# V of an attention kernel through a padded DRAM buffer by head group, in place of four SBUF blocks

## The chip, the cores and the metric

One core of a Trainium2 chip. The metric is device time in microseconds (us) of one execution. The kernel before took 3974.69 us (median of 3 runs, 3971.6 to 3993.35).

## The reference

Two layers, each an attention block and then an MLP block with Mish, on S = 2048 rows of D = 512, in float32 throughout:

```python
x = A_x
x = x + _A_ref(_layernorm(x, axis=-1), A_wqkv, A_wo)
x = x + _B_ref(_layernorm(x, axis=-1), B_w1, B_b1, B_w2)
x = x + _A_ref(_layernorm(x, axis=-1), A_wqkv, A_wo)
x = x + _B_ref(_layernorm(x, axis=-1), B_w1, B_b1, B_w2)
...
# _A_ref: H = 32 heads of Dh = 16
qkv = (lambda x, *d: x.transpose(*d))((x @ wqkv).reshape(B, S, 3, H, Dh), 2, 0, 3, 1, 4)
scores = jnp.einsum("bhqd,bhkd->bhqk", q, k) * (Dh ** -0.5)
p = _softmax(scores, axis=-1)
o = jnp.einsum("bhqk,bhkd->bhqd", p, v)
return (lambda x, *d: x.transpose(*d))(o, 0, 2, 1, 3).reshape(B, S, D) @ wo
```

## The kernel before

**Blocks.** Most of SBUF is one pool, `blk`: 22 blocks of 8 KB a partition (`NBLK`, handed out by `b8`). Normalized x, weights, K and Q of a head group, V, attention output, residuals and exponentials all take their tiles from it. Which block a tile gets, and so which earlier reader it waits for, is settled when the program is built; a scheduler then also sets the order on each engine, except where the code chains PE's instructions one behind the other (`pe`), as it does from the first max matmul of an attention to its end.

**QK stage.** `qkv` computes Q and K transposed, splits each result into a high and a low part, and writes them to DRAM (`scr`, 512 KB a tile, issued by ACT). `prep_qk(g)` loads K and Q of head group g back from there, by SP: two `ks` and two `qs` blocks for a group of four heads (`HG`); there are eight groups (`NG`).

**V stage.** `qkv` ends with V: 16 row tiles of 128 rows (c = 0..3, t = 0..3), each 12 matmuls into a PSUM bank, and one ACT copy. Four tiles share one block `v{l}{c}`. The four blocks live to the last head group, since `prep_v(g)` takes from them the columns of its group: into a fresh block `va` that POOL first zeroes (L232) and gives a column of ones a head (L233, which yields the softmax denominators), it copies four pieces (L235). Each head has 32 columns there (`VW`), 16 of them V.

**Attention.** `run` goes through 512 steps a layer: eight groups of 64, each 4 blocks of 512 queries (qb) by 16 key tiles (kt). A step is four heads' scores for one kt and qb. `CYCLE` writes out the order by hand: P, a pair of score matmuls `sp` and one exponential over both (L312); S, a single score `ss` and its exponential (L322); M, a max matmul `pm` and its maximum on DVE (L265), which run 24 steps ahead (`AHEAD`); v, the product of exponentials and va (`pv`, L339), two steps behind the scores. Each tile `p` holds three heads' exponentials and takes one block; its number is that of its first head, so `p0486` is layer 0, head 486, and the tile before is `p0483`. The maxima of 16 steps are folded on DVE (`nm`, L272), transposed on PE (`nmt`, L282), split on DVE (`np`) and loaded into rows of `qs` by eight small DMAs of SP (L289).

**Group switch.** In steps 32 to 63 of a group `prep_qk` loads the next group's four blocks; at step 48 `prep_v` fills the next va. The old group's ks, qs and va come free when its last steps have been done. During these last 16 steps the pool holds ks and qs of two groups, two va, four output blocks and four v blocks. In the last group the v blocks are done with, and weights of Wo and W1 and the residuals come in instead.

Of the kernel before, what the change touches and what calls it, by code (L numbers as in the profile page):

```python
# [9 lines left out]
F32 = mybir.dt.float32  # L10
F32R = mybir.dt.float32r
BF16 = mybir.dt.bfloat16
AF = mybir.ActivationFunctionType
# [5 lines left out]
P = 128  # L19
S, D, H, DH, F = 2048, 512, 32, 16, 1792  # L20
NCH = 4
CW = S // NCH
KT = D // P
NKT = S // P
FT = F // P
HG = 4
NG = H // HG
VW = 32
# [21 lines left out]
def kernel(ctx: ExitStack, tc: tile.TileContext, x, wqkv, wo, w1, b1, w2, out):  # L50
    nc = tc.nc
# [7 lines left out]
    dram = ctx.enter_context(tc.tile_pool(name="dram", bufs=1, space=DRAM))  # L59
# [13 lines left out]
    def b8(shape, dt, name):  # L73
        return blk.tile(shape, dt, tag="blk", name=name)
# [13 lines left out]
    def pbank(tag, name):  # L88
        if tag == "s":
            return banks["s"].tile([P, 512], F32, tag=tag, name=name, bufs=3)  # L90
        return ps.tile([P, 512], F32, tag=tag, name=name, bufs=1)
# [32 lines left out]
    def split_psum(hi, lo, src):  # L124
        nc.scalar.activation(hi, src, AF.Copy)
        nc.vector.tensor_tensor(lo, src, hi.bitcast(F32), op=ALU.subtract)

    def mm3(acc, pairs, first=True, last=True, pe=lambda ins: ins):
        n = len(pairs)
        for i, (ah, al, bh, bl) in enumerate(pairs):  # L130
            pe(nc.tensor.matmul(acc, ah, bh, start=first and i == 0, stop=False))  # L131
            pe(nc.tensor.matmul(acc, ah, bl, start=False, stop=False))  # L132
            pe(nc.tensor.matmul(acc, al, bh, start=False, stop=last and i == n - 1))  # L133
# [45 lines left out]
    class Attention:  # L179
        def __init__(self, l, scr):  # L180
            self.l, self.scr = l, scr
            self.vall = {}
            self.qk, self.va, self.mxs, self.pts, self.accs = {}, {}, {}, [], {}
            self.singles, self.full = 0, None
            self.ost = None
            self.later = []
            self.chained, self.running, self.last = False, False, None
# [41 lines left out]

        def prep_v(self, g):  # L230
            va = b8([P, NKT, HG, VW], F32, f"va{self.l}{g}")
            nc.gpsimd.memset(va, 0.0)  # L232
            nc.gpsimd.memset(va[:, :, :, DH : DH + 1], 1.0)  # L233
            for c in range(NCH):
                nc.gpsimd.tensor_copy(  # L235
                    va[:, ts(c, NCH), :, 0:DH],
                    self.vall[c][:, :, ts(g, HG * DH)].rearrange("p t (h d) -> p t h d", d=DH),
                )
            self.va[g] = va

# [166 lines left out]
    def load_qkv(l, wts, which, **kw):  # L407
        for j in which:
            if j < 4:
                wts[j] = load_cols(wqkv, j, f"wqk{l}{j}", **kw)  # L410
            else:
                wts[j] = load_rows(wqkv[:, 2 * D : 3 * D], j - 4, f"wv{l}{j}", **kw)

    def qkv(l, wts, tt, order, late):
        scr = [dram.tile([2, P, S], F32R, name=f"scr{l}{m}") for m in range(2 * NCH)]
        att = Attention(l, scr)
        ahead = [0]

        def some_max():
            if ahead[0] < AHEAD:  # L420
                att.chained = True
                att.tick()
                for n in range(2):
                    att.max_mm(ahead[0], n)
                ahead[0] += 1

        done = 0
        for m, c in order:
            if c not in tt:
                late()  # L430
            w = wts[m // 2]
            pt = tmp.tile([P, 2, CW], F32R, tag="raw", name=f"pt{l}{m}{c}", bufs=3)
            th, tl = tt[c]
            acc = pbank("s", f"qk{l}{c}{m}")
            mm3(
                acc,
                [(w[:, 0, k, ts(m % 2, P)], w[:, 1, k, ts(m % 2, P)], th[:, k], tl[:, k]) for k in range(KT)],
                pe=att.pe,
            )
            split_psum(pt[:, 0], pt[:, 1], acc)  # L440
            nc.scalar.dma_start(
                scr[m][:, :, ts(c, CW)].bitcast(F32).rearrange("a p n -> p a n"), pt.bitcast(F32)
            )
            if (m, c) == (5, 3) and 4 not in wts:
                load_qkv(l, wts, (4, 5), behind=True)
            if m in (0, 4):
                done += 1
                if done == 2 * NCH:
                    for _ in att.prep_qk(0):
                        pass  # L450
            elif done == 2 * NCH and m in MAX_M:
                some_max()
        for c in range(NCH):
            th, tl = tt[c]
            v = b8([P, NCH, D], F32, f"v{l}{c}")
            for t in range(NCH):
                acc = pbank("s", f"va{l}{c}{t}")
                mm3(
                    acc,
                    [  # L460
                        (th[:, k, ts(t, P)], tl[:, k, ts(t, P)], wts[4 + k // 2][:, 0, k % 2], wts[4 + k // 2][:, 1, k % 2])
                        for k in range(KT)
                    ],
                    pe=att.pe,
                )
                nc.scalar.activation(v[:, t, :], acc, AF.Copy)
                some_max()
            att.vall[c] = v
        return att

    def wo_parts(l, c, ost, wot, x2, pe, tail):
# [122 lines left out]
    for l in range(2):  # L594
        if l == 0:
            order = [(0, 0), (4, 0), (0, 1), (4, 1), (1, 0), (0, 2), (4, 2), (1, 1), (0, 3), (4, 3)]
        else:
            order = [(0, 0), (0, 1), (0, 2), (4, 0), (4, 1), (4, 2), (1, 0), (0, 3), (4, 3)]
        order += [(m, c) for m in (1, 5, 2, 6, 3, 7) for c in range(NCH) if (m, c) not in order]
        att = qkv(l, wts, tt, order, late)  # L600
        wot, w1t, w2t, x2s, tts = [], [], [], [], {}
        xsrc = x if l == 0 else xs
# [81 lines left out]
```

## Time and profile before

| | us |
|---|---|
| runs | 3971.6, 3974.69, 3993.35 |
| profiled execution, its own time | 3967.7 |
| its span, first to last instruction | 3965.9 |
| mean granted TensorE clock | 0.961 |
| DMA traffic, mean over the span | 34 GB/s |

A line of the costliest groups reads: source line, engine, operation, output and inputs, shapes, count; then busy time in us and mean ns of one; then the idle time of the engine just before them, and what ended most of it. In the waits the three numbers are total us, times, and the longest in us. A row of the windows holds the stretch in us from the span's start, its length, then busy us and number of instructions of PE, PEld, DVE, ACT and POOL, then the granted clock, the share of the DMA engines and GB/s; with one line of the kernel selected, only the engines that run it appear.

The DMA queues: that of SP (q1) moved 89.17 MB in 42768 packets, that of ACT (q10) 40.90 MB in 22240. POOL is busy for 494.2 us of the span, and 28.9 us of that are the 16 zeroings of va (L232), 23.1 us the 64 copies (L235).

### The profile page before, as it was taken

The numbers are of one execution on the slowest core, as the hardware profiler recorded it, in microseconds if no ns is written. First come the engines' busy times: TensorE is split into PE (matmuls) and PEld (weight loads), VectorE is DVE, ScalarE is ACT, GpSimd is POOL, SyncE is SP. The second block draws the span as 40 slices with busy tenths as digits, with TensorE's granted clock in tenths as the row PEclk, the third lists the DMA queues.
The fourth block names the chain that finished last, engine by engine and source line by source line (L and its number), as shares of the span: only waits on it lengthen the run. The fifth ranks groups of instructions, "written<-read, shape, count | busy, mean of one in ns | idle before, by whom it ended". The sixth has DMA issues, their size and how long they took to land.

```text
span 3965.9 us, 70422 instructions
## 1 busy us (share of the span) xinstructions
PE 3802.0 (96%) x29504; PEld 2090.7 (53%) x29504; DVE 3093.7 (78%) x3266; ACT 2517.8 (63%) x3445; POOL 494.2 (12%) x401
## 2 busy tenths in 40 slices
PE   7999999999999999999999999999999999999999
PEld 5744444444444444588776444444444444446887
DVE  5689989687988898466656799897998979965655
ACT  2177777576776777544431777776777767774444
POOL 1000000000000011254420000000000000204545
PEclk9999999697998999999999999998999989999999
DMA  6220111110010201100033201111110202101000
GB/s 186 107 34 10 26 18 18 17 18 18 18 28 8 34 12 44 53 7 22 22 123 128 34 7 29 18 18 18 18 30 6 34 2 34 34 23 59 11 11 22
DMA packets 65326, 134.58 MB, mean 34 GB/s; under 512 B 12272, under 2 KB 26608, under 8 KB 58864
## 3 DMA queue, kind: packets, MB, share of 16 engines
q1 hardware_dynamic: 42768, 89.17, 10.6%
q10 hardware_dynamic: 22240, 40.90, 2.9%
q8 instruction: 232, 3.80, 0.4%
q14 instruction: 86, 0.70, 0.1%
HBM read 85.99 MB, written 41.94 MB: 32 GB/s over the span
## 4 chain that ended last, share of the span: by engine, by line
PE 44%; DVE 4%; ACT 2%; POOL 1%; DMA 1%; issue 1%; POOLq 0%; DVEq 0%; ACTq 0%; SPq 0%
PE pv L339 13%; PE pm L261 9%; PE sp L311 6%; PE ss L321 4%; DVE mxv L265 2%; PE mo L133 1%; PE h L131 1%; PE h L133 1%; PE h L132 1%; PE mo L131 1%; PE mo L132 1%; ACT p L312 1%; POOL hb L532 1%; DVE al L533 1%; PE qk L131 1%
## 5 line engine op out<-in xcount | busy, mean ns | idle before, releaser
L265 DVE TENSOR_REDUCE mxv<-pm 128x2 f32<-128x1024 f32 x2048 | 2430.9, 1221 | 392.0 <-PE pm L261 380.6
L312 ACT ACTIVATE p<-sp 128x1024 f32<-128x1024 f32 x1366 | 1398.5, 1024 | 737.8 <-PE sp L311 642.8
L339 PE MATMUL pv<-p,va 128*32 128x256 f32 x16384 | 1221.2, 402 | 0.3
L261 PE MATMUL pm<-ks,qs 48*128 48x512 f32 x4096 | 954.0, 464 | 40.2 <-DVE mxv L265 38.0
L322 ACT ACTIVATE p<-ss 128x512 f32<-128x512 f32 x1364 | 809.2, 593 | 11.4 <-PE ss L321 11.4
L339 PEld LDWEIGHTS pv<-p,va 128*32 128x32 f32 x16384 | 403.3, 111 | 613.0 <-issue 488.2
L311 PE MATMUL sp<-qs,ks 50*128 50x512 f32 x2732 | 645.6, 467 | 69.6 <-ACT p L312 64.2
L261 PEld LDWEIGHTS pm<-ks,qs 48*128 48x128 f32 x4096 | 397.9, 192 | 449.4 <-issue 279.3
L321 PE MATMUL ss<-qs,ks 50*128 50x512 f32 x1364 | 561.2, 411 | 0.0
L311 PEld LDWEIGHTS sp<-qs,ks 50*128 50x128 f32 x2732 | 267.2, 190 | 400.3 <-ACT p L312 318.3
L232 POOL MEMSET va<- 128x2048 f32 x16 | 28.9, 1809 | 2390.8 <-ACT p L312 900.1
L321 PEld LDWEIGHTS ss<-qs,ks 50*128 50x128 f32 x1364 | 264.4, 194 | 90.5 <-ACT p L322 58.1
L529 POOL TENSOR_TENSOR hb<-hb,he 128x512 f32<-128x512 f32 x112 | 157.1, 1403 | 186.2 <-DVE he L526 179.4
L131 PE MATMUL mo<-w,ah 128*128 128x512 f32 x448 | 179.4, 400 | 0.8 <-DVE ah L531 0.7
L131 PE MATMUL h<-thm,w 128*128 128x512 f32 x448 | 176.0, 393 | 1.6 <-ACT hb L523 1.6
L132 PE MATMUL mo<-w,ah 128*128 128x512 f32 x448 | 177.3, 396 | 0.0
L532 POOL TENSOR_TENSOR hb<-hb,hr 128x512 f32<-128x512 f32 x112 | 160.1, 1430 | 136.4 <-DVE ah L531 115.4
L133 PE MATMUL h<-thm,w 128*128 128x512 f32 x448 | 175.6, 392 | 0.0
L132 PE MATMUL h<-tlm,w 128*128 128x512 f32 x448 | 175.2, 391 | 0.0
L533 DVE TENSOR_TENSOR al<-hb,ah 128x512 fp32r<-128x512 f32 x112 | 110.8, 989 | 81.9 <-POOL hb L532 81.9
L133 PE MATMUL mo<-w,al 128*128 128x512 f32 x448 | 163.7, 402 | 7.8 <-DVE al L533 7.8
L527 ACT ACTIVATE hr<-he 128x512 f32<-128x512 f32 x112 | 70.9, 633 | 156.9 <-DVE he L526 78.3
(168 smaller groups left out, 2777.2 us busy)
## 6 DMA issues: line engine op xcount, KB each, us to landing
scr<-pt ACTq DMA_DIRECT2D x64, 512.0 KB
qs<-scr SPq DMA_DIRECT2D x192, 128.0 KB
ks<-scr SPq DMA_DIRECT2D x192, 128.0 KB
qs<-np SPq DMA_DIRECT2D x512, 2.0 KB
x<-in_A_x_dram SPq DMA_DIRECT2D x7, 1024.0 KB
xs<-x SPq DMA_DIRECT2D x4, 1024.0 KB
x<-xs SPq DMA_DIRECT2D x4, 1024.0 KB
out_dram<-x SPq DMA_DIRECT2D x3, 1024.0 KB
```

The lines of the kernel that those rows point to most:

```text
L131: pe(nc.tensor.matmul(acc, ah, bh, start=first and i == 0, stop=False))
L132: pe(nc.tensor.matmul(acc, ah, bl, start=False, stop=False))
L133: pe(nc.tensor.matmul(acc, al, bh, start=False, stop=last and i == n - 1))
L261: nc.tensor.matmul(pm[:, e], qs[u][rows, q0 : q0 + P], ks[u][rows, ts(n, 512)], start=True, stop=True)
L265: nc.vector.tensor_reduce(self.mxs[b][:, 2 * u : 2 * u + 2, qt, n], pm, axis=AX.X, op=ALU.max)
L311: self.pe(nc.tensor.matmul(sp[:, e], k, q, start=True, stop=True))
L312: nc.scalar.activation(self.pts[-1][:, 0:n], sp[:, 0:n], AF.Exp, scale=SCALE)
L321: self.pe(nc.tensor.matmul(sp, k, q, start=True, stop=True))
L322: nc.scalar.activation(self.pts[i // 3][:, 2], sp, AF.Exp, scale=SCALE)
L339: nc.tensor.matmul(acc[ts(h, VW), cols], va[:, kt, h, :], self.pts[j][:, e, cols], start=kt == 0 and half == 0, stop=kt == NKT - 1, skip_g ...
L529: nc.gpsimd.tensor_tensor(hb, hb, e, op=ALU.mult)
L532: nc.gpsimd.tensor_tensor(hb, hb, r, op=ALU.mult)
```

## The change

V no longer stays in SBUF. Two row tiles at a time go into a block `v` that POOL has zeroed and given its columns of ones, with every head already padded to 32 columns; two DMAs of SP write them into a DRAM buffer `vscr`, laid out by head group. `prep_v` becomes four DMA loads by SP. A layer now has eight short-lived v blocks in the V stage and none behind it.

```diff
-            self.vall = {}
+            self.vscr = dram.tile([NG, P, NKT, HG * VW], F32, name=f"vscr{l}")
...
         def prep_v(self, g):
             va = b8([P, NKT, HG, VW], F32, f"va{self.l}{g}")
-            nc.gpsimd.memset(va, 0.0)
-            nc.gpsimd.memset(va[:, :, :, DH : DH + 1], 1.0)
             for c in range(NCH):
-                nc.gpsimd.tensor_copy(
-                    va[:, ts(c, NCH), :, 0:DH],
-                    self.vall[c][:, :, ts(g, HG * DH)].rearrange("p t (h d) -> p t h d", d=DH),
+                nc.sync.dma_start(
+                    va[:, ts(c, NCH)].rearrange("p k h d -> p k (h d)"), self.vscr[g, :, ts(c, NCH)]
                 )
...
-            v = b8([P, NCH, D], F32, f"v{l}{c}")
             for t in range(NCH):
+                if t % 2 == 0:
+                    v = b8([P, 2, H, VW], F32, f"v{l}{c}{t}")
+                    nc.gpsimd.memset(v, 0.0)
+                    nc.gpsimd.memset(v[:, :, :, DH : DH + 1], 1.0)
...
-                nc.scalar.activation(v[:, t, :], acc, AF.Copy)
+                nc.scalar.activation(v[:, t % 2, :, 0:DH], acc.rearrange("p (h d) -> p h d", d=DH), AF.Copy)
+                if t % 2:
+                    k0 = c * NCH + t - 1
+                    for k in range(2):
+                        nc.sync.dma_start(
+                            att.vscr[:, :, k0 + k].rearrange("g p n -> p g n"),
+                            v[:, k].rearrange("p (g h) d -> p g (h d)", g=NG),
+                        )
                 some_max()
-            att.vall[c] = v
```

The order on PE is the same before and after, instruction for instruction. These rows of PE before stand near the end of layer 0's second head group (steps 121 to 126 of the layer, a switch); the first name is what is written, behind the arrow what is read:

```order
L339 MATMUL pv07_4673<-p0486_4887,va01_2745 32x256
L339 MATMUL pv07_4673<-p0489_4903,va01_2745 32x256 x3
L261 MATMUL pm0908_4962<-ks020_3437,qs020_3438 128x512 x2
L311 MATMUL sp0498_4966<-qs011_2003,ks011_2002 128x512 x2
L261 MATMUL pm0909_4971<-ks020_3437,qs020_3438 128x512 x2
L321 MATMUL ss0500_4975<-qs010_1587,ks010_1586 128x512
L339 MATMUL pv07_4673<-p0486_4887,va01_2745 32x256
L339 MATMUL pv07_4673<-p0489_4903,va01_2745 32x256 x3
L311 MATMUL sp0501_4982<-qs010_1587,ks010_1586 128x512
```

Nothing moves here; what is changed is the block into which the exponential of `sp0498` writes: that of `p0486` before, that of `p0474` after.

On POOL, at the end of layer 0's QK stage (`wv` is the low part of V's weights, `x..r` a raw load), before:

```order
L110 TENSOR_TENSOR wv04_644<-wv04r_645,wv04_644 128x1024
L110 TENSOR_TENSOR wv05_649<-wv05r_650,wv05_649 128x1024
L232 MEMSET va00_1367 128x2048
L233 MEMSET va00_1367 128x64
L235 COPY va00_1367<-v00_1057 128x16x16
```

and after:

```order
L110 TENSOR_TENSOR wv04_645<-wv04r_646,wv04_645 128x1024
L456 MEMSET v000_1058 128x2048
L456 MEMSET v002_1121 128x2048
L456 MEMSET v010_1170 128x2048
L456 MEMSET v012_1219 128x2048
L456 MEMSET v020_1268 128x2048
L456 MEMSET v022_1301 128x2048
L110 TENSOR_TENSOR wv05_650<-wv05r_651,wv05_650 128x1024
L457 MEMSET v000_1058 128x64
```

Six zeroings stand ahead of the second split now; the zeroing of va and the copies out of v are gone, here and at every switch.

On SP after, from the V stage to the first attention steps of layer 0 (`qs000<-np00` are max rows; before, the rows with `vscr` were not there, and the others stood in the same order):

```order
L102 DMA w100r_14620<-in_B_w1_dram 128x4x256
L287 DMA qs000_512<-np00_1102 1x4x128
L471 DMA vscr0_340<-v000_1058 128x8x128
L287 DMA qs000_512<-np00_1102 1x4x128 x3
L287 DMA qs001_528<-np00_1102 1x4x128 x4
L471 DMA vscr0_340<-v002_1121 128x8x128 x2
L234 DMA va00_1404<-vscr0_340 128x512
L471 DMA vscr0_340<-v010_1170 128x8x128 x2
L471 DMA vscr0_340<-v012_1219 128x8x128 x2
L234 DMA va00_1404<-vscr0_340 128x512
```

The writes of a quarter of V and the load of that quarter for group 0 alternate. At each later switch four loads of va stand between the max rows of two query blocks.

On DVE the only thing that moves is the place of some folds. For the third query block of the fourth group of layer 0, before:

```order
L265 TENSOR_REDUCE mxv014_7150<-pm014115_7607 128x2
L272 TENSOR_REDUCE nm014_7611<-mxv014_7150 128x16
L265 TENSOR_REDUCE mxv015_7619<-pm01500_7620 128x2
L284 CAST np014_7637<-nmt014_7635 16x128
L285 TENSOR_TENSOR np014_7637<-nmt014_7635,np014_7637 16x128
```

and after:

```order
L263 TENSOR_REDUCE mxv014_7179<-pm014115_7636 128x2
L263 TENSOR_REDUCE mxv015_7648<-pm01500_7649 128x2
L270 TENSOR_REDUCE nm014_7640<-mxv014_7179 128x16
L282 CAST np014_7666<-nmt014_7664 16x128
L283 TENSOR_TENSOR np014_7666<-nmt014_7664,np014_7666 16x128
```

The fold stands one maximum later. Of the 64 folds of the program 8 stand so before and 12 after.

More of the change, by code (lines that the diff above doesn't have):

```diff
@@ L181, in __init__ @@
             self.l, self.scr = l, scr
-            self.vall = {}
-            self.qk, self.va, self.mxs, self.pts, self.accs = {}, {}, {}, [], {}
+            self.vscr = dram.tile([NG, P, NKT, HG * VW], F32, name=f"vscr{l}")
+            self.va = {}
+            self.qk, self.mxs, self.pts, self.accs = {}, {}, [], {}
             self.singles, self.full = 0, None
```

## The prediction

> **What bounds the kernel now.** I read the page first, then the waits of PE, then one group switch of the attention row by row, then windows from switch to switch.
>
> ```profile
> PE 3802.0 (96%) x29504; PEld 2090.7 (53%) x29504; DVE 3093.7 (78%) x3266; ACT 2517.8 (63%) x3445; POOL 494.2 (12%) x401
> ...
> PEclk9999999697998999999999999998999989999999
> ```
>
> PE fills the span, so what counts is PE's idle time and the clock that it is granted: the PEclk row dips in the attention stages. The largest wait of PE on one line, from its waits:
>
> ```profile
> PE sp L311 <- ACT p L312: 64.2, 73, 1.4
> ...
> PE nmt L282 <- DVE nm L272: 3.9, 4, 1.0
> ```
>
> The score matmuls `sp` wait 64.2 us for an exponential to empty its PSUM tile. Why the exponential is late stands in the costliest groups, and in the timeline of one such wait in the last quarter of a head group:
>
> ```profile
> L312 ACT ACTIVATE p<-sp 128x1024 f32<-128x1024 f32 x1366 | 1398.5, 1024 | 737.8 <-PE sp L311 642.8 <-PE pv L339 87.1 <-PE pm L261 4.0
> L339 PE MATMUL pv<-p,va 128*32 128x256 f32 x16384 | 1221.2, 402 | 0.3
> ```
>
> ```profile
> 498.22 0.64 PE L339 MATMUL pv<-p,va 128*32 128x256 f32 x8
> 498.94 1.02 ACT L312 ACTIVATE p<-sp 128x1024 f32<-128x1024 f32 x1 [1.29 <-PE pv L339]
> ...
> 500.02 0.50 PE L311 MATMUL sp<-qs,ks 50*128 50x512 f32 x2 [1.15 <-ACT p L312]
> ```
>
> ACT idles 1.29 us for `pv`, that is for a block: the exponential's output tile is the block of an earlier one that `pv` still reads. PE's next `sp` then idles 1.15 us. The order rows above say why: with four blocks, exponential 498 gets the block of 486 (four tiles of three heads back), and the last `pv` reading 486 stands on PE behind `sp0498`. Four is what the pool leaves at a switch: 22 blocks less 8 (ks and qs of two groups), 2 va, 4 output tiles and 4 v.
>
> Now the attention from one zeroing of va to the next, `pv` rows alone, layer 0 and then layer 1. The pv count gives the steps: 16384 records over 1024 steps are 16 a step.
>
> ```profile
> 323.90:493.60 169.70, 74.16 (x1040) 24.87 (x1040) 1.00 0.13 21
> 493.60:669.70 176.10, 75.01 (x1040) 25.04 (x1040) 0.99 0.12 20
> 669.70:873.30 203.60, 87.42 (x1008) 26.84 (x1008) 0.80 0.11 17
> 873.30:1065.80 192.50, 83.08 (x1024) 26.35 (x1024) 0.87 0.10 18
> 1065.80:1242.10 176.30, 75.02 (x1040) 25.04 (x1040) 0.99 0.12 20
> 1242.10:1428.70 186.60, 79.41 (x1008) 25.59 (x1008) 0.89 0.11 19
> ```
>
> ```profile
> 2315.20:2484.90 169.70, 74.16 (x1040) 24.87 (x1040) 1.00 0.13 21
> 2484.90:2662.20 177.30, 75.87 (x1040) 25.22 (x1040) 0.98 0.12 20
> 2662.20:2848.80 186.60, 79.57 (x1008) 25.62 (x1008) 0.89 0.11 19
> 2848.80:3021.10 172.30, 72.87 (x1024) 24.55 (x1024) 1.00 0.12 20
> 3021.10:3195.40 174.30, 74.15 (x1040) 24.87 (x1040) 1.00 0.12 20
> 3195.40:3380.60 185.20, 78.72 (x1008) 25.53 (x1008) 0.91 0.12 19
> ```
>
> The first window of each layer holds no such wait (at the first switch the fourth output block is not yet taken, so five are left): 65 steps in 169.70 us, 2.611 us a step, at full clock, the same in both layers. The other five of each layer hold a tight switch, and each is slower. Windows cut at the switch show where:
>
> ```profile
> 669.70:732.00 62.30, 55.93 (x392) 24.65 (x393) 39.68 (x38) 32.70 (x45) 3.29 (x6) 0.71 0.00 1
> 732.00:873.30 141.30, 139.24 (x1144) 62.52 (x1142) 115.05 (x110) 96.80 (x129) 0.00 (x0) 0.84 0.15 24
> ...
> 1242.10:1305.60 63.50, 57.44 (x392) 25.34 (x393) 39.48 (x38) 32.56 (x44) 3.28 (x6) 0.68 0.00 1
> 1305.60:1428.70 123.10, 120.17 (x1144) 55.68 (x1143) 114.90 (x110) 96.57 (x129) 0.00 (x0) 1.00 0.17 28
> ```
>
> Idle time and the lower clock (0.71, 0.68) begin in the switch; in the second case the rest of the group runs at 1.00, in the first the drop lasts on into it (0.84).
>
> **The change part by part.** *Stalls removed.* The four v blocks live only through the V stage, so a switch leaves 8 blocks: exponential 498 reuses 474, whose `pv` is far ahead on PE. PE's own order does not change. If all windows run at the clean rate, six windows of a layer (385 steps) take 385 x 2.611 = 1005.2 us. They take now:
>
> ```profile
> 323.90:493.60 169.70, 166.77 (x1583) 77.13 (x1583) 159.00 (x151) 133.83 (x179) 3.34 (x7) 1.00 0.13 21
> ...
> sum 1104.80, PE 1060.09 PEld 484.41 DVE 943.43 ACT 790.97 POOL 19.92; mean PE 176.68 PEld 80.74 DVE 157.24 ACT 131.83 POOL 3.32
> ```
>
> ```profile
> sum 1065.40, PE 1019.97 PEld 469.29 DVE 942.80 ACT 790.68 POOL 19.96; mean PE 169.99 PEld 78.22 DVE 157.13 ACT 131.78 POOL 3.33
> ```
>
> That is 99.6 us too much in layer 0 and 60.2 in layer 1, **159.9 us**. Of it PE idle: (1104.80 - 1060.09) + (1065.40 - 1019.97) = 90.1 us, less twelve times the clean 2.93, is 55.0 us. The other **104.9 us** is PE running at a lower clock. Next in line is DVE, 159.00 of the clean 169.70 us: it fits, and the clean windows already contain its waits.
>
> Whether the 104.9 us goes too is the main choice. For it: the drops lie in the tight switches, while switches without stalls show 1.00; and load alone does not do it, since the MLP keeps PE busier at full clock:
>
> ```profile
> 1700.00:1900.00 200.00, 198.16 (x874) 160.01 (x873) 126.39 (x184) 94.99 (x147) 100.60 (x72) 1.00 0.03 11
> ```
>
> So I take the drop as a consequence of the stalls and let it go whole: -159.9. [...]
>
> *V stage.* POOL zeroes eight v tiles there instead of one va, six of them ahead of the second wv split:
>
> ```profile
> 102.43 2.37 POOL L110 TENSOR_TENSOR wv<-wv05r,wv 128x1024 fp32r<-128x1024 f32 x1 [1.12 <-ACT wv L106]
> 104.73 1.82 POOL L232 MEMSET va<- 128x2048 f32 x1
> ```
>
> ```profile
> 152.38 0.60 ACT L466 ACTIVATE v<-va 128x512 f32<-128x512 f32 x1 [3.02 <-PE va L133]
> ```
>
> 6 x 1.82 = 10.9 us moves that split's end from 104.8 to about 116; the first V tile is done at 152.4, so over 30 us cover it. ACT's strided copy is not in the trace: between nothing and twice 0.60 us, under the 3.02 us that ACT idles before each. Taken as 0.
>
> Sixteen writes of 512 KB a layer and the read back for group 0 are new. The nearest rows are the QK stage, which writes such tiles (`scr<-pt`, 15 in this window, in pieces four times longer), and the two longest transfers on the chain around 2070 us:
>
> ```profile
> 100.00:149.00 49.00, 48.86 (x207) 33.80 (x208) 36.93 (x39) 9.55 (x16) 5.66 (x4) 0.95 0.42 163
> ```
>
> ```profile
> 2070.28 7.44 DMA scr<-pt
> 2077.74 6.68 DMA ks<-scr
> ```
>
> There 15 writes took 0.42 x 49 / 15 = 1.4 us of all DMA engines each and PE stayed 48.86 of 49 us busy. Low end: hidden, 0. High end: cost by pieces, 4 x 1.4 = 5.5 us a write, one after another from 153 us on. The last quarter of va is then there at 153 + 16 x 5.5 + 6.7 = 248 us. PE needs it at step 14; the first window above begins at step 48, so step 14 is near 323.9 - 34 x 2.611 = 235: 13 us a layer, 26 us. I take 0, by the QK stage, whose bytes and pace are the same.
>
> *Group switch.* POOL's zeroing and four copies go; POOL waits there, nobody waits for it. Instead SP issues four loads of 256 KB at step 48; they wait for a block, and queued behind them are the next block's 2 KB max rows, used some 8 steps (21 us) later. va is needed at step 66, 47 us after; the longest read above is 6.7 us. 0.
>
> *DVE order.* The max fold `nm` stands one `mxv` late at 12 places, at 8 before. Four of the 8 cost PE 3.9 us, so 4 more places x half x 1 us: +2 us (ends 0 and 12 - 3.9 = 8).
>
> **Sum**, from the profiled execution (3967.7 us, span 3965.9 and 1.8 around it): 3967.7 - 159.9 + 2 = **3810 us**. The median shown, 3974.7, is 7.0 us above that execution; where clock drops go away, the runs' differences in them go too, so I forecast 3810 and not 3817.
>
> **The rivals.** *The clock drops stay.* Only the idle 55.0 us goes: 3967.7 - 55.0 + 2 = 3915 us. For it: the gaps are short, and a drop outlasts its switch (0.84 from 732 us on). Against: layer 1's fourth and fifth windows have stalls and no drop, but none has a drop without stalls. [...] Between the two, a part stays: 3840 to 3880.
>
> *V comes late (slower).* If a write takes W, va's last quarter is there at 153 + 16 W + 6.7, and PE stands from 235 us on until then, in both layers. At W = 7.44, the longest row, it is 279 us: 44 us a layer, 88 in all, 3898. To eat the whole 159.9 it takes 80 us a layer, W = 9.7 us; beyond, the kernel is slower, at 11 us (101 us a layer) about 4010. Against: the QK stage moves the same bytes at 3.3 us a tile.
>
> *The blocks do not reach the exponentials* (earlier loads of ks and qs take them): stalls and drops stay, 3970. Against: a group's needs are fixed by the code, 8 + 2 + 4, whenever they load.
>
> **How the numbers follow.** Forecast (3798 to 3842) 0.72; part of the drops stays 0.08; all stay 0.12; no effect 0.05; V late and slower 0.03. The range 3798 to 3880 holds the first two, 0.80, to the ends of the V stage and DVE terms (3810 + 26 + 6); the low end lets a third of the 12 x 2.93 us of idle in the clean windows go as well, 12 us. This kernel's measurement tells about 0.5% from no change; faster by more 0.92, within 0.05, slower 0.03.
>
> **What would show it.** Right: every stretch of 64 steps near 167 us at PEclk 1.00; ACT's wait on `pv` (87.1 us) almost gone, PE's on `p` near 10 us; PE busy near 3700 us. Wrong: PEclk under 0.9 at a switch without idle PE (the clock has its own cause); PE waiting on a DMA into va at steps 2 to 14 (V late); `sp` still waiting at the switches (blocks).

## The result, and the profile after

The changed kernel takes 3809.82 us (median of 4 runs, 3802.49 to 3818.48); the kernel before, run beside it, 3973.14 us (median of 4). The ratio of the two is 0.9635 with a 95% interval of 0.9534 to 0.9737: faster by 3.6%. The forecast was 3810 us. The profiled execution took 3818.48 us (span 3816.7), against 3967.7 before: 149.2 us less.

The page of the changed kernel, the shares of the engines, the row of the granted clock and the group of the exponentials. Read them against the same rows of before: PE's busy time falls by 94.4 us although it runs the same 29504 matmuls, and the dips of the clock row in the attention stages are gone.

```profile
PE 3707.6 (97%) x29504; PEld 2055.3 (54%) x29504; DVE 3087.6 (81%) x3266; ACT 2517.6 (66%) x3445; POOL 473.1 (12%) x337
...
PEclk9989999999999999999999999999999999999999
...
L310 ACT ACTIVATE p<-sp 128x1024 f32<-128x1024 f32 x1366 | 1398.5, 1024 | 594.4 <-PE sp L309 577.4
```

Before, 87.1 us of ACT's idle time stood behind `pv`; that releaser is not among those listed now. The waits of PE (engine and line, whom it waited for: us in all, times, the longest) show that its wait for an exponential went from 64.2 us to 8.4, and that the largest wait left is the one for DVE's maxima:

```profile
PE pm L259 <- DVE mxv L263: 37.7, 76, 0.7
PE sp L309 <- ACT p L310: 8.4, 21, 0.7
...
PE nmt L280 <- DVE nm L270: 5.8, 6, 1.0
```

The six windows of layer 0 from switch to switch (from step 48 of a group to step 48 of the next, 64 steps), `pv` rows alone: start and end, length, busy time of PE, PEld and ACT, granted clock, DMA share and rate.

```profile
335.40:502.30 166.90, 73.13 (x1031) 24.71 (x1032) 2.41 (x4) 1.00 0.14 27
502.30:668.70 166.40, 72.83 (x1024) 24.29 (x1016) 2.40 (x4) 1.00 0.15 27
668.70:836.80 168.10, 72.88 (x1024) 24.55 (x1024) 2.40 (x4) 1.00 0.14 27
836.80:1003.80 167.00, 73.23 (x1032) 24.71 (x1032) 2.41 (x4) 1.00 0.14 27
1003.80:1170.20 166.40, 72.73 (x1024) 24.29 (x1016) 2.40 (x4) 1.00 0.15 27
1170.20:1338.20 168.00, 72.88 (x1024) 24.55 (x1024) 2.41 (x4) 1.00 0.15 27
```

Every window takes 166.4 to 168.1 us at a clock of 1.00, and so do the six of layer 1 (166.7 to 168.0 us); before, the five tight ones of each layer took 172.3 to 203.6 us. The sums of the same six windows with all engines, layer 0 and then layer 1, split the gain into idle time and clock:

```profile
sum 1002.80, PE 984.05 PEld 455.76 DVE 937.25 ACT 787.97 POOL 0.00; mean PE 164.01 PEld 75.96 DVE 156.21 ACT 131.33 POOL 0.00
```

```profile
sum 1004.20, PE 983.28 PEld 455.86 DVE 937.31 ACT 787.65 POOL 0.00; mean PE 163.88 PEld 75.98 DVE 156.22 ACT 131.28 POOL 0.00
```

The 768 steps take 2007.0 us. Before, 770 steps took 2170.2, so 768 of them (less two clean steps of 2.611) 2165.0: **158.0 us** gained. PE's idle time in these windows fell from 90.1 to 39.7 us, which is 50.4; the other 107.6 us is less busy time for the same matmuls, which run at full clock now.

The V stage of layer 0, the stretch from the first V tile to the attention, first after and then before (busy time of PE, PEld, DVE, ACT, POOL; clock; DMA share; GB/s):

```profile
152.00:200.00 48.00, 47.75 (x212) 35.46 (x212) 19.40 (x19) 8.96 (x15) 0.00 (x0) 1.00 0.68 203
```

```profile
152.00:200.00 48.00, 47.75 (x212) 35.29 (x211) 19.70 (x20) 8.97 (x15) 1.20 (x3) 1.00 0.10 34
```

The DMA engines now move 203 GB/s there, six times as much, and PE is busy for the same 47.75 of 48 us (in layer 1 48.75 of 49 us, after and before). ACT's strided copy costs nothing either: 0.60 us a copy in both, 8.96 against 8.97 us of ACT in this stretch.

What was lost elsewhere is at the start of each layer's attention. The first 25 us of it, layer 0 and layer 1, after and then before:

```profile
202.00:227.00 25.00, 24.18 (x131) 10.60 (x129) 15.46 (x13) 13.61 (x18) 0.00 (x0) 0.52 0.31 65
2099.00:2124.00 25.00, 23.64 (x147) 10.45 (x146) 15.94 (x14) 14.85 (x20) 0.00 (x0) 0.66 0.34 72
```

```profile
202.20:227.20 25.00, 24.13 (x182) 10.71 (x179) 20.28 (x18) 18.21 (x24) 0.00 (x0) 0.80 0.21 33
2194.60:2219.60 25.00, 23.45 (x185) 10.79 (x183) 21.41 (x19) 18.38 (x26) 0.40 (x1) 0.86 0.21 33
```

PE's idle time is nearly the same (0.82 and 1.36 us, before 0.87 and 1.55), but its clock is lower (0.52 and 0.66, before 0.80 and 0.86), and in the same 25 us it gets through 131 and 147 matmuls where it got through 182 and 185. At the clean rate (1563 matmuls in 166.90 us) these 89 are 9.5 us, about the 8.8 us that lie between the 158.0 us of the twelve windows and the 149.2 us of the whole.

### The profile page after: what moved, and what is told of

It is laid out like the page before. It is cut to its first block, busy times and chain, and to the rows that moved or that the text cites. A ratio compares the mean times of both kernels' runs of the same rounds, so it can differ in the third digit from the quotient of the medians.

```text
span 3816.7 us, 70470 instructions
## 1 busy us (share of the span) xinstructions
PE 3707.6 (97%) x29504; PEld 2055.3 (54%) x29504; DVE 3087.6 (81%) x3266; ACT 2517.6 (66%) x3445; POOL 473.1 (12%) x337
## 4 chain that ended last, share of the span: by engine, by line
PE 45%; DVE 5%; ACT 2%; POOL 1%; DMA 1%; issue 1%; DVEq 0%; POOLq 0%; SPq 0%; ACTq 0%
PE pv L337 13%; PE pm L259 9%; PE sp L309 6%; PE ss L319 4%; DVE mxv L263 2%; PE mo L133 1%; PE h L131 1%; PE h L133 1%; PE h L132 1%; PE mo L131 1%; PE mo L132 1%; POOL hb L539 1%; DVE al L540 1%; ACT p L310 1%; PE qk L131 1%
## 5 line engine op out<-in xcount | busy, mean ns | idle before, releaser
L337 PE MATMUL pv<-p,va 128*32 128x256 f32 x16384 | 1174.9, 389 | 0.0
L259 PE MATMUL pm<-ks,qs 48*128 48x512 f32 x4096 | 931.0, 453 | 41.1 <-DVE mxv L263 37.7
L337 PEld LDWEIGHTS pv<-p,va 128*32 128x32 f32 x16384 | 394.6, 109 | 580.9 <-issue 442.2
L309 PE MATMUL sp<-qs,ks 50*128 50x512 f32 x2732 | 629.6, 456 | 14.7 <-ACT p L310 8.4
L259 PEld LDWEIGHTS pm<-ks,qs 48*128 48x128 f32 x4096 | 386.4, 186 | 436.0 <-issue 275.7
L319 PE MATMUL ss<-qs,ks 50*128 50x512 f32 x1364 | 546.4, 401 | 0.0
L319 PEld LDWEIGHTS ss<-qs,ks 50*128 50x128 f32 x1364 | 255.6, 187 | 89.1 <-ACT p L320 60.3
```

The source lines that it names most:

```text
L259: nc.tensor.matmul(pm[:, e], qs[u][rows, q0 : q0 + P], ks[u][rows, ts(n, 512)], start=True, stop=True)
L309: self.pe(nc.tensor.matmul(sp[:, e], k, q, start=True, stop=True))
L319: self.pe(nc.tensor.matmul(sp, k, q, start=True, stop=True))
L337: nc.tensor.matmul(acc[ts(h, VW), cols], va[:, kt, h, :], self.pts[j][:, e, cols], start=kt == 0 and half == 0, stop=kt == NKT - 1, skip_g ...
```

## The experiments

The theory (the forecast's): at a switch four free blocks make an exponential wait for `pv`; each such wait stalls PE for 1.15 us, and the stalls are what brings the clock down. The rivals: the gain comes from what the change takes off POOL and SBUF at the switch (zeroing and copies); the clock has a cause of its own at the switch; the new path of V has a price that the gain hides. Experiments 1 to 4 ran on one chip beside 19 runs of the kernel before (median 3953.09 us), 5 to 7 on another beside 11 (3965.2 us). The changed kernel itself ran beside neither, so a difference to its 3809.82 us spans two sets of runs. None of the experiments leaves out or changes any part of the computation.

**1 and 2. Take the blocks back, and only the blocks.** The changed kernel, in which POOL writes 16 columns of each of four blocks at step 1 of a layer and touches one of them again at step 432, so that no exponential can have them in between. Four blocks are left at a switch then, as before; with three held, five. V still goes through DRAM, and POOL still has nothing to zero or to copy at a switch.

```diff
+                    if s == 1:
+                        held = [b8([P, 16], F32, f"hold{self.l}{s}{n}") for n in range(4)]
+                        for h in held:
+                            nc.gpsimd.memset(h, 0.0)
+                    if s == STEPS - GSTEPS - NKT:
+                        for h in held:
+                            nc.gpsimd.tensor_tensor(h[:, 0:1], h[:, 0:1], self.pts[-1][:, 0, 0:1], op=ALU.add)
```

The second has `range(3)` in its place.

> The changed kernel, with four more blocks taken out of the pool from step 1 of an attention to step 432 (a small POOL op writes them, a small one reads them at the end): at a group switch four blocks are left for exponentials, as before the change; V still goes through DRAM. Theory (blocks run short, PE stalls, the clock falls with the stalls): the whole loss comes back, 3915 to 3995 us, about 50 waits of ACT L310 on pv, PE idle 55 us more than after, PEclk under 0.95 at several switches. Rival A (the clock falls by a cause of its own, tied to POOL's zeroing and copying at the switch): only the idle time comes back, 3865 us, PEclk 1.00 at the switches. Rival B (the gain is POOL's work taken off the switch, not the blocks): 3810 us, no waits on pv.

> The same with three blocks held, so that five are left at a switch. Theory: five are enough, since the last pv that reads a block then stands ahead of the score matmul on PE; 3802 to 3820 us, no wait of an exponential on pv at a switch, PEclk 1.00 there. Rival C (every block counts, the gain grows with each): about a quarter to half of the gain is lost, 3850 to 3890 us.

Four held: 3962.68 us (10 runs), ratio to before 1.0016 [0.9972, 1.006]. Three held: 3812.69 us (4 runs), 0.9646 [0.9581, 0.9712]. One block is worth 150 us. The waits of ACT with four held, and windows over a switch and the stretch behind it, PE alone:

```profile
ACT p L310 <- PE pv L337: 86.2, 50, 3.3
```

```profile
680.00:738.40 58.40, 52.04 (x348) 0.68 0.02 5
738.40:780.30 41.90, 41.18 (x397) 1.00 0.24 40
```

Fifty waits are back, as many as before, and so is the low clock at the switch. With three held, PE's wait for exponentials and the same switch:

```profile
PE sp L309 <- ACT p L310: 8.3, 21, 0.7
```

```profile
669.00:711.20 42.20, 41.08 (x393) 1.00 0.03 11
```

No wait for `pv` is listed for ACT here. Since the first of these kernels lacks POOL's work at the switch and has V's new path, and still runs like the kernel before, the gain comes from neither, and the two together change the time by too little for this measurement.

**3. The gain without the change.** The kernel before, with its four v blocks, fills va at step 62 of a group and not at 48. Until then the block of the second va is free, so five are left. Of the 50 waits 4 remain by the order of the program, one in the third and one in the sixth group of each layer.

```diff
-                    if s % GSTEPS == GSTEPS - NKT and s // GSTEPS + 1 < NG:
+                    if s % GSTEPS == GSTEPS - 2 and s // GSTEPS + 1 < NG:
```

> The kernel before (V in four SBUF blocks, POOL zeroes and copies), with one constant changed: the next group's va is filled at step 62 of a group and not at step 48, so that five blocks are left for exponentials until then. Theory: nearly the whole gain without the change, 3805 to 3850 us, at most 1 wait on pv a switch. Rival A: idle gone, drops stay, about 3915 us. Rival B: 3970 us, as before.

3823.81 us (4 runs: 3811.60, 3811.56, 3836.03, 3858.66), ratio 0.9693 [0.9609, 0.9776]. ACT's waits for `pv`, and PE's for exponentials:

```profile
ACT p L312 <- PE pv L339: 5.3, 4, 1.3
```

```profile
PE sp L311 <- ACT p L312: 13.8, 28, 1.2
```

Four waits, as the program's order says. One moved line gives nearly the whole gain with V where it was. Two of the four runs are some 24 and 47 us longer than the others, at a mean granted clock of 0.988 and 0.980 against 0.995; whether the four stalls left cost the clock there isn't known, since the profiled run (3811.60) shows no drop at a switch.

**4. Move the shortage away from the switch.** The changed kernel with five blocks held in steps 28 to 44 of the second to the sixth group, ahead of the filling of the next va. Of the 22 blocks 8 are ks and qs there, 1 va, 4 output tiles and 5 held: four are left. Outside of these steps, and so at the switch, it has as many blocks as the change gives it.

```diff
+                    if s % GSTEPS == 28 and 1 <= s // GSTEPS <= 5:
+                        held = [b8([P, 16], F32, f"hold{self.l}{s}{n}") for n in range(5)]
+                        for h in held:
+                            nc.gpsimd.memset(h, 0.0)
+                    if s % GSTEPS == 44 and 1 <= s // GSTEPS <= 5:
+                        for h in held:
+                            nc.gpsimd.tensor_tensor(h[:, 0:1], h[:, 0:1], self.pts[-1][:, 0, 0:1], op=ALU.add)
```

> The changed kernel, with five blocks held from step 28 to step 44 of groups 1 to 5 of each layer, when the next K and Q have come in: four are left for exponentials in the middle of a group, and eight again at its switch. Theory: the five stalls of 1.15 us move to the middle of the group and the clock drops move with them; idle 55 us more than after, PEclk under 1.00 in the middle of several groups and 1.00 at the switches, 3870 to 3990 us. Rival A (the drops belong to the switch): idle alone, 3865 us, PEclk 1.00 in the middle.

3963.34 us (10 runs), 1.0011 [0.9963, 1.0058]. The profiled execution, at 3991.57 us the longest of the ten, serves here for the places and not for the time; the other nine (3928.0 to 3983.66 us) have a mean granted clock of 0.958 to 0.974, against 0.991 to 0.995 of the changed kernel, so the low clock isn't that execution's alone. ACT's waits, and three windows of the fourth group of layer 0: its first half, its third quarter, in which the blocks are held (the holding begins four steps before it), and the fourth quarter, which is the switch.

```profile
ACT p L310 <- PE pv L337: 91.2, 52, 3.3
```

```profile
738.90:823.90 85.00, 81.47 (x778) 37.61 (x776) 79.10 (x75) 65.82 (x88) 0.56 (x5) 1.00 0.24 40
823.90:891.90 68.00, 63.08 (x393) 27.29 (x393) 38.74 (x37) 32.64 (x45) 0.76 (x5) 0.60 0.05 17
891.90:933.50 41.60, 40.85 (x397) 18.87 (x394) 39.09 (x38) 32.77 (x44) 0.00 (x0) 1.00 0.01 2
```

The stalls went to the middle of the group, and the low clock with them: 0.60 there, 1.00 in the switch. So in this run the switch without stalls doesn't lower the clock.

**5. Half of the stalls.** The kernel before with va filled at step 56; by the order of the program 24 of the 50 waits remain.

```diff
-                    if s % GSTEPS == GSTEPS - NKT and s // GSTEPS + 1 < NG:
+                    if s % GSTEPS == GSTEPS - 8 and s // GSTEPS + 1 < NG:
```

> The kernel before, with va filled at step 56 of a group: 24 of the 50 stalls of 1.15 us are left in the built program, two or three at each of the ten switches, within 20 us. Idle time 24 x 1.15 = 28 us above the changed kernel. If each stall is as likely to cost the clock as it was before (105 us over 50 stalls, 2.1 us each), 3810 + 28 + 50 = 3888 us. If the clock needs all five close together, 3838 us and PEclk 1.00 at the switches. If the drop is all or nothing a switch (any stall sets it off), 3810 + 28 + 100 = 3938 us.

3866.7 us (4 runs), 0.9788 [0.9731, 0.9845].

```profile
ACT p L312 <- PE pv L339: 37.8, 24, 3.3
```

Above the changed kernel's 3809.8 us that is 56.9 us, 2.4 us for each of 24 stalls. With 50 (experiment 1) it is 152.9 us, 3.1 each, and with 52 (experiment 4) 153.5, 3.0 each. The price of a stall is between two and three times its 1.15 us, and about a fifth less when there are half as many. The median meets none of the three times of the expectation. The four runs (3862.68 to 3890.61 us) lie well off two of them: that the clock costs nothing until all five stalls of a switch come together (3838 us), and that any stall sets off the whole drop (3938 us). A price in proportion (3888 us) lies within the runs, 21 us above their median.

**6 and 7. What is left: the start of the attention, and the zeroing.** In the changed kernel PE stands still twice, 0.69 and 0.71 us, as the attention of layer 0 begins (as it did before), and the clock drops behind it (1.00 from 201 to 203 us, 0.50 from 203 to 226). Experiment 6 takes the last V tile of a layer apart and places it into step 0 as filling. Experiment 7 lets DVE zero v instead of POOL.

```diff
-        def prep_v(self, g):
+        def prep_v(self, g, part=range(NCH)):
...
-                    for item in CYCLE[s % 3]:
+                    for n, item in enumerate(CYCLE[s % 3]):
+                        if s == 0 and n in (1, 3):
+                            next(self.rest, None)
+                            if n == 3:
+                                self.prep_v(0, [NCH - 1])
...
+                if (c, t) == (NCH - 1, NCH - 1):
+                    att.rest = tile_parts(tag="acc")
+                    continue
```

> The changed kernel, with the last row tile of V (its 12 matmuls in two halves) moved from the end of the V stage into step 0 of the attention, where PE waits 0.7 us twice for the first exponentials, and where the clock falls to half for 24 us in layer 0 and 17 us in layer 1. The same work is done. If the fall comes from these waits, PEclk in the first 40 us goes up and 8 to 16 us go: 3795 to 3802 us. If it belongs to the start of the score matmuls, or the waits only move by a step, no change: 3805 to 3815 us.

```diff
-                    nc.gpsimd.memset(v, 0.0)
-                    nc.gpsimd.memset(v[:, :, :, DH : DH + 1], 1.0)
+                    nc.vector.memset(v, 0.0)
+                    nc.vector.memset(v[:, :, :, DH : DH + 1], 1.0)
```

> The changed kernel, with v zeroed by VectorE and not by POOL. In the changed kernel four zeroings on POOL (1953.7 to 1961.3 us) run beside the last layer norm ahead of layer 1, whose row tiles (L158) then take 1.04 and 1.50 us on DVE where they took 0.55 before, and PE waits 3.47 us there for 2.01 before. If POOL's zeroing slows DVE, the two tiles take 0.55 us again and the gap is 2.0 us; the time as a whole moves by under 3 us, 3805 to 3815. If it is something else in that place (the transfers), they stay long.

Experiment 6: 3815.26 us (6 runs), 0.964 [0.9597, 0.9682], no different from the changed kernel. The first 25 us of the two attentions, PE alone:

```profile
194.50:219.50 25.00, 23.90 (x197) 1.00 0.37 94
2094.00:2119.00 25.00, 24.00 (x135) 0.67 0.37 90
```

Layer 0 keeps its clock, layer 1 loses it still (its next 25 us are at 0.79; in all that is 27.3 us at half clock, against 17.1 in the changed kernel's profiled execution), although the program is the same in both. The filling didn't end the waits: PE stands still for 0.48 and 0.56 us in layer 0 and for 0.47 and 0.54 in layer 1, and layer 1 has one more, for a copy of V:

```profile
2093.40 0.57 PE L310 MATMUL sp<-qs,ks 50*128 50x512 f32 x2 [0.75 <-ACT v L474]
```

So this experiment shows neither that the waits set the clock here nor that they don't; what sets it at this place stays open.

Experiment 7: 3836.97 us (4 runs, 3819.18 to 3871.24), 0.9685 [0.9619, 0.9752]. The median is some 27 us above that of the changed kernel and 22 above that of experiment 6, which ran beside it (3804.16 to 3819.91), so the expected 3805 to 3815 us was missed; the intervals of the ratios overlap. The reason for trying it is in the timeline of the changed kernel ahead of layer 1, where POOL zeroes four tiles while DVE normalises; the same rows of before, where POOL has nothing to do there, follow.

```profile
1953.68 7.64 POOL L456 MEMSET v<- 128x2048 f32 x4
...
1954.77 1.04 DVE L158 TENSOR_SCALAR xnq<-x,mvq,rsq 128x512 f32<-128x512 f32 x1 [0.99 <-PE tpq L166]
...
1956.33 1.50 DVE L158 TENSOR_SCALAR xnq<-x,mvq,rsq 128x512 f32<-128x512 f32 x1
...
1958.58 1.94 PE L166 MATMUL tpq<-ident,xnq 128*128 128x128 f32 x8 [3.47 <-DVE tlq L126]
```

```profile
2048.54 0.55 DVE L158 TENSOR_SCALAR xnq<-x,mvq,rsq 128x512 f32<-128x512 f32 x1 [0.99 <-PE tpq L166]
...
2049.60 0.54 DVE L158 TENSOR_SCALAR xnq<-x,mvq,rsq 128x512 f32<-128x512 f32 x1
...
2050.89 1.23 PE L166 MATMUL tpq<-ident,xnq 128*128 128x128 f32 x8 [2.01 <-DVE tlq L126]
```

The same DVE instruction takes 1.04 and 1.50 us beside the zeroing, and PE's gap behind it grows from 2.01 to 3.47 us. With the zeroing on DVE it is 0.55 and 0.54 us again and the gap 2.01, so it was POOL's zeroing. But DVE pays for it elsewhere. The timeline of DVE in experiment 7, and PE's wait that follows it:

```profile
2018.94 1.76 DVE L456 MEMSET v<- 128x2048 f32 x1 [0.38 <-DMA ks<-ones]
2021.08 1.76 DVE L456 MEMSET v<- 128x2048 f32 x1 [0.38 <-issue]
2022.77 0.63 DVE L126 TENSOR_TENSOR pt<-qk,pt 128x512 fp32r<-128x512 f32 x1
```

```profile
2023.45 0.80 PE L131 MATMUL qk<-thq,wqk 128*128 128x512 f32 x1 [5.77 <-DVE pt L126]
```

The split `pt` stands behind the zeroings on DVE, and PE waits 5.77 us for it; in the changed kernel its whole wait for `pt` at this place of the code is 7.1 us over both layers, here 19.8, 12.7 us more. This execution (3871.24 us) is 52.8 us longer than the changed kernel's profiled one; most of the rest lies at the starts of the two attentions, which take 65.2 us each from the start of the first exponential to that of the 43rd (some 16 steps), against 49.3 and 47.4. The first 50 us in layer 0, all engines:

```profile
213.30:238.30 25.00, 23.79 (x133) 10.32 (x132) 15.46 (x13) 13.72 (x18) 0.00 (x0) 0.57 0.28 65
238.30:263.30 25.00, 24.71 (x133) 10.30 (x135) 14.11 (x15) 11.56 (x15) 0.00 (x0) 0.50 0.20 33
```

After 25 us it is still at 0.50. Why it comes back later here than in the changed kernel wasn't found. No experiment beat the changed kernel.

## Why the prediction was right, step by step

- **Blocks.** Four left made the waits, more than four end them. Experiments 1 and 2 show that the step is between four and five; the eight that the change leaves are three more than are needed. The rival that the blocks don't reach the exponentials falls.
- **Stalls removed, -55.0 us.** Measured -50.4 us in the twelve windows. The clean window that the sum used had 2.93 us of idle PE; the changed kernel's have 3.3 on the mean (39.7 / 12).
- **Clock, -104.9 us.** Measured -107.6. This was the main choice, and experiment 4 shows its reason: the low clock goes where the stalls go (0.60 in the middle of a group, 1.00 at its switch). The rival "the clock drops stay" (3915 us) falls, and "a part stays" (3840 to 3880) with it, since all twelve windows are at 1.00. That the gaps are short, an argument for the first of them, is true and did not help it: PE's waits for an exponential in the kernel before are 1.4 us at the longest, and at two of its switches the clock was 0.71 and 0.68.
- **V stage, 0.** Held: 47.75 us of PE in the 48 us stretch, before and after, with no wait of PE for a load of va behind it. The high end of the range (5.5 us a write, and the last quarter of va there at 248 us) was far off: SP issued that quarter's load at 204.3 us, behind the last write, and pieces a quarter as long didn't make the transfers visible to PE. The rival that ended slower, V late, falls; experiment 1 bounds V's path and POOL's relief together, from 0.3% gained to 0.6% lost.
- **DVE order, +2 us.** PE's waits for the fold `nm` went from 3.9 us (4 times) to 5.8 (6 times): +1.9.
- **Not in the sum.** The attention's start (9.5 us more in the profiled execution) and POOL's zeroing beside DVE's normalising (1.5 us of PE's gap). The prediction counted the zeroings as moved on POOL, and saw only the queue behind them there. The start varies by itself: experiments 1 and 4 have the changed kernel's V stage and showed, in their first 25 us, PE alone, the clocks below, from 0.52 to 0.86.

```profile
201.10:226.10 25.00, 23.81 (x182) 0.80 0.30 65
2167.60:2192.60 25.00, 23.67 (x148) 0.66 0.28 65
```

```profile
202.00:227.00 25.00, 24.18 (x131) 0.52 0.29 65
2185.00:2210.00 25.00, 23.64 (x185) 0.86 0.33 66
```

So the profiled execution is 8.5 us above the forecast, while the other three runs, at a mean granted clock of 0.993 to 0.995 against its 0.991, are 7.9 to 16.0 us shorter than it. That the median meets the forecast within a microsecond is partly luck; the terms agree to about 5 us.

## What to carry to other kernels

Where a pool's blocks limit a stream, count the free ones at the tightest place and look on the reading engine's order for the last reader of the block that comes next: here the fifth block is worth 150 us, and the sixth to the eighth nothing (3812.69 us with five, 3809.82 with eight). In this kernel, whose stream on TensorE is otherwise full, a stall of 1.15 us cost two to three times its length (2.4 to 3.1 us): the clock that went with it cost as much as the wait with 24 stalls, and over one and a half times as much with 50. Before data is moved elsewhere to make room, see whether it can be moved in time: filling va 14 steps later brought nearly the same gain with one constant.

## What was unexpected of the hardware

**The clock halved behind a stall of 1.15 us, and full work didn't bring it back at once.** Windows of 3.4 us of the kernel before, around a switch, PE alone (length, busy time, granted clock):

```profile
674.80:678.20 3.40, 2.25 (x25) 1.00 0.02 5
678.20:681.60 3.40, 3.40 (x23) 0.50 0.00 0
...
688.40:691.80 3.40, 2.25 (x26) 1.00 0.00 0
691.80:695.20 3.40, 3.40 (x38) 1.00 0.02 5
```

```profile
740.00:743.40 3.40, 3.40 (x25) 0.50 0.02 5
```

The first window holds one stall of 1.15 us, and the next runs at 0.50; the third holds a stall of the same length, and the clock stays at 1.00. So a stall in the window is not all that decides, and what else does is open. That the stalls bring the drops shows in their sum, and in where the drops lie: at the switch 0.68 with four blocks held and 1.00 with three (experiments 1 and 2), and 0.60 in the middle of a group (experiment 4). The drop that begins at 698.7 us in this trace lasts 78.5 us, all of it at 0.50; at 740 us the last stall, in the row below, is over 12 us old, PE is busy without a pause, and the clock is still at half.

```profile
727.24 0.80 PE L311 MATMUL sp<-qs,ks 50*128 50x512 f32 x2 [1.16 <-ACT p L312]
```

**POOL's zeroing slowed VectorE.** 0.55 us became 1.04 and 1.50 us beside POOL's zeroings of some 1.9 us each (7.64 us for four). That the one slows the other, experiment 7 shows: with the zeroing on DVE the two instructions took 0.55 and 0.54 us again. The longest delay here, 0.96 us, is half of a zeroing; by what path the one delays the other is not shown.
